# Pairs of 256-token expert tiles merged into tiles of 512 in a dilated attention and mixture-of-experts kernel

## The chip, the cores and the metric

The kernel runs on one core of one Trainium2 chip. The time is the device time of that core in microseconds (us), from the first to the last instruction with what lies around them; the median of three runs is given. The engines are PE (TensorE, matmuls; "PEld" is its weight load), DVE (VectorE), ACT (ScalarE), POOL (GpSimd) and SP (SyncE, which here only issues DMAs).

## The reference

Attention over 8 batches, 8 heads and 576 tokens gives rows `x` of 512 features; each token then goes through one of 8 experts. A token takes the expert of its own largest logit, or the one of the token before it, by a local gate. Only the second part matters here:

```
for b in range(B):                      # B, S, D, E, F = 8, 576, 512, 8, 1024
    prev_e = -1
    for s in range(S):
        fresh_e = int(np.argmax(logits[b, s]))
        if s == 0 or local_gate[b, s] < 0.5:  e = fresh_e
        else:                                 e = prev_e if prev_e >= 0 else fresh_e
        prev_e = e
        p = softmax(logits[b, s])
        h = np.maximum(x[b, s] @ w1[e], 0.0)
        out[b, s] = p[e] * (h @ w2[e])
```

All of it is f32. A matmul of f32 operands is two passes (two MATMUL records and two LDWEIGHTS records) in the trace.

## The kernel before, in words

**Stages.** Attention and routing take the first 181 us or so. While they run, each token's expert and place within that expert are worked out. Two units of 256 tokens (`EARLY`, `FIRST`) are formed from the first half of the batches; the rest is cut up once all tokens are routed (`count(True)`, `table`, `tokens`, lines 628 to 763). From there on the kernel is a list of *units*, `units` (lines 765 to 775): 14 of kind "pair" (256 tokens of one expert), 4 "full" (128 tokens), 1 "half" (64) and 3 "few" (32), in an order fixed at build time; only which tokens and which expert a unit holds is known at run time. With the two early ones there are 24 units.

**One unit.** `gather` fetches the token rows with indirect DMAs issued by POOL (two for each 128 tokens, into one of four `xg` buffers). `features` turns them with PE transposes and copies them to `xe` with ACT. `hidden` computes relu(x·w1) with the features on the partitions: the weights are PE's stationary operand, the tokens are the moving columns. `output` computes h·w2 with the tokens stationary and 256 of the 512 output features moving; the result is scaled by the gate into a `y` tile (three buffers), and `send` scatters 128 rows by an indirect DMA issued by POOL. Each send waits for the landing of the send before it, since both write `out`.

**Seven products in place of eight.** A pair is split 2×2 and multiplied by the Strassen-Winograd scheme in `chain` (lines 897 to 921). It needs sums of blocks of both operands: `sums_left` and `sums_right`, four DVE additions each. For the first product these are the sums of w1's blocks (`sums[0]`, 128x1024 each) and of the tokens (`xc`, 128x256); for the second, of h (`hc`, 128x512) and of w2's blocks (`sums[1]`, 128x1024). In `hidden` one of the seven products is 8 matmuls with 128 moving columns; in `output` it is 4 matmuls with 256.

**Order of the work.** PE, DVE, POOL and SP run in the order in which the program is written. The loop at line 1234 does, for unit u: `hidden(u)`, then `features(u + 1)`, `gather(u + 2)`, `output(u - 1)`. DVE's sums are slipped in between products, one or two at each `yield` of `chain` (`work_gap`, lines 817 to 821): during `hidden(u)` those for the output of u - 1 (`both`, line 1206), during `output(u - 1)` those of w1 for u + 1. The routing's last steps (`count`, `table`, `tokens`) are slipped in the same way between the products of unit 1's `hidden`, one step at each gap, each a short chain of DVE operations on 128x8 tiles.

**Weights.** There are three places for a unit's w1 and w2 (`raw1`, `raw2`, 2 MB each): pairs alternate between the first two, all other units use the third. A place is loaded for its next user as soon as its last reader is done (`weights`, lines 786 to 800; called from `run_hidden`, line 1193, and `run_output`, line 1201). The load is skipped where the place already holds the expert.

Of the kernel before, what the change touches and what calls it, by code (L numbers as in the profile page):

```python
# [81 lines left out]
PAIRS, FULL, HALF, FEWS = 14, 4, 1, 3  # L82
C_FULL, C_HALF, C_FEW = (2 * MOST + k * E for k in range(3))
COLS = C_FEW + E

# [133 lines left out]
def whole(ctx, tc, exact, bad, qk, v, wgl, w1, w2, con, adm, msk, qmk, out, cst, wg, ones, warm):  # L219
# [32 lines left out]
    def bank(shape, name):  # L252
        return banks.tile(shape, F32, name=name, tag="bank")
# [374 lines left out]
    def count(late):  # L628
# [11 lines left out]
        if late:  # L640
            ki, kf = number("ki", I32), number("kf")
            nc.vector.tensor_scalar(ki, ni, 5, None, Alu.logical_shift_right)
            nc.vector.tensor_scalar(ni, ni, float(FEW), None, Alu.add)
            tiles["over"] = over = sm.tile([1, 5], F32, name="over_late")
            most = sm.tile([1, 1], F32, name="most")
            nc.vector.tensor_reduce(most, cn[0:1], axis=AX.X, op=Alu.max)
            nc.vector.tensor_scalar(over[:, 4:], most, float(SEGS * P), None, Alu.is_gt)
# [3 lines left out]
        if late:  # L651

            nc.vector.tensor_copy(kf, ki)
            nc.vector.scalar_tensor_tensor(kf, nf, -8.0, kf, Alu.mult, Alu.add)
            full, half, few = number("full"), number("half"), number("few")
            nc.vector.tensor_scalar(full, kf, 3.0, None, Alu.is_ge)
            nc.vector.scalar_tensor_tensor(kf, full, -4.0, kf, Alu.mult, Alu.add)
            nc.vector.tensor_scalar(half, kf, 2.0, None, Alu.is_ge)
            nc.vector.tensor_scalar(few, kf, 1.0, None, Alu.is_equal)
            left = number("left")  # L660
            nc.vector.tensor_tensor(left, nf, tiles["done"], op=Alu.subtract)
            parts = [left, full, half, few]
# [6 lines left out]
        if late:  # L669
            for k, most in enumerate((PAIRS, FULL, HALF, FEWS)):  # L670
                nc.vector.tensor_scalar(over[:, k:k + 1], ends[k][0:1, E - 1:], float(most), None, Alu.is_gt)
        if not late:
            tiles["done"] = done = number("done")
            nc.vector.tensor_scalar(done, befs[0], -1.0, float(FIRST), Alu.mult, Alu.add)
            nc.vector.tensor_scalar(done, done, 0.0, None, Alu.max)
            nc.vector.tensor_tensor(done, done, nf, op=Alu.min)
            first, ends = None, [(done, befs[0], 0)]
        else:
            first = tiles["done"]
            nc.vector.tensor_tensor(befs[0], befs[0], first, op=Alu.subtract)  # L680
            ends = [(nf, befs[0], 0), (full, befs[1], C_FULL), (half, befs[2], C_HALF), (few, befs[3], C_FEW)]
        cols = COLS if late else 2 * FIRST
        tiles["chosen", late] = []
        for turn in range(PASSES if exact and late else 1):
# [7 lines left out]
            nc.vector.tensor_scalar(to, befs[0], 2.0, seg1, Alu.mult, Alu.add)  # L692
            if late:
                nc.vector.tensor_scalar(twice, first, 2.0, None, Alu.mult)
                nc.vector.scalar_tensor_tensor(to, twice, seg, to, Alu.is_le, Alu.mult)
# [28 lines left out]
    def tokens(late):  # L724
# [33 lines left out]
        if late:  # L758
            tiles["side"] = side = sm.tile([P, 2 * E], I32, name="side")
            for k, parts in enumerate((P // ROW, P // FEW)):  # L760
# [4 lines left out]
    n_pairs, *n_others = (MOST, E, E, E) if exact else (PAIRS, FULL, HALF, FEWS)  # L765
    others = [(kind, c + k) for k in range(max(n_others))
              for kind, c, most in zip(("full", "half", "few"), (C_FULL, C_HALF, C_FEW), n_others) if k < most]
    n_others = len(others)
    units = [dict(kind="pair" if i else "plain", col=2 * i, slot=i, late=False) for i in range(FIRST)]
    for k in range(n_pairs):  # L770
        i = k // 2 + k % 2 * (n_pairs // 2)
        units.append(dict(kind="pair", col=2 * i, slot=k % 2, late=True))
        while len(others) > min(n_others, max(n_others * (n_pairs - 1 - k) // (n_pairs - 2), k < n_pairs - 1)):
            kind, col = others.pop(0)
            units.append(dict(kind=kind, col=col, slot=2, late=True))
    NU = len(units)

    def of_unit(u, what, j=0, rows=P):
        return tiles[what, units[u]["late"]][:rows, units[u]["col"] + j:units[u]["col"] + j + 1]
# [43 lines left out]
    def now(push):  # L823
        for f in push:
            f()
# [32 lines left out]
    def tiles_of(u):  # L858
        return 2 if units[u]["kind"] in ("pair", "plain") else 1
# [21 lines left out]
    def features(u):  # L881
        kind = units[u]["kind"]
        rows = rows_in(u)
        xe[u] = mw.tile([P, DK, 2 * P], F32, name="xe")
        for j in range(tiles_of(u)):
            x = xg.pop((u, j)).rearrange("p g f -> p (g f)")
            tp = bank([P, DK, P], "tp")
            for kk in range(DK):
                nc.tensor.transpose(tp[:, kk, :rows], x[:rows, kk * P:(kk + 1) * P], ident[:rows, :rows])
            nc.scalar.copy(xe[u][:, :, j * P:j * P + rows], tp[:, :, :rows])  # L890
        if kind == "pair":
            xc[u] = mw.tile([P, 4, DK // 2, P], F32, name="xc", bufs=1)
            return sums_right(xc[u], *(xe[u][:, 2 * k:2 * k + 2, j * P:(j + 1) * P]
                                       for k in range(2) for j in range(2)))
        return []
# [27 lines left out]
    def hidden(u):  # L923
        i, kind = units[u]["slot"], units[u]["kind"]
        ht[u] = h = stage.tile([P, FK, 2 * P], F32, name="h", bufs=2)
# [36 lines left out]
        xyz = [bank([P, FK // 2, P], "hp") for _ in range(3)]  # L962

        def at(k):
            return h[:, k // 2 * FK // 2:(k // 2 + 1) * FK // 2, k % 2 * P:(k % 2 + 1) * P]

        def product(to, a, b, first):
            for m in range(FK // 2):
                for kk in range(DK // 2):
                    nc.tensor.matmul(to[:, m], lhsT=a[:, m, kk], rhs=b[:, kk], start=first and m == 0 and kk == 0,  # L970
                                     stop=(kk == DK // 2 - 1), skip_group_check=True)

        def keep(k, of):
            nc.scalar.copy(at((0, 1, 3)[k]), of)  # L974

        def finish(k, of):
            if k == 2:
                nc.scalar.activation(at(2), of, Act.Relu)
            else:
                nc.vector.tensor_tensor(at(k), of, at(k), op=Alu.add)  # L980
                nc.scalar.activation(at(k), at(k), Act.Relu)  # L981

        yield from chain((lambda i_, k: quarter(w, i_, k, False), lambda s: sums[0][:, s]),
                         (lambda k, j: x[:, 2 * k:2 * k + 2, j * P:(j + 1) * P], lambda s: xc[u][:, s]),
                         *xyz, product, keep, finish)
        units[u]["sums"] = sums_left(hc, at(0), at(2), at(1), at(3))
# [15 lines left out]
    def output(u):  # L1002
# [43 lines left out]
        xyz = [bank([P, D // 2], "yp") for _ in range(3)]  # L1046
        ys = [stage.tile([P, D], F32, name="y", bufs=3) for _ in range(2)]
        half = D // 2

        def product(to, a, b, first):  # L1050
            for m in range(FK // 2):
                nc.tensor.matmul(to, lhsT=a[:, m], rhs=b[:, m], start=first and m == 0,  # L1052
                                 stop=(m == FK // 2 - 1), skip_group_check=True)

        def at(k):
            return ys[k // 2][:, k % 2 * half:(k % 2 + 1) * half]

        def keep(k, of):
            k = (0, 1, 3)[k]
            nc.scalar.activation(at(k), of, Act.Copy, scale=of_unit(u, "gate", k // 2))  # L1060

        def finish(k, of):
            if k == 2:
                nc.scalar.activation(at(k), of, Act.Copy, scale=of_unit(u, "gate", 1))
                send(ys[1], u, 1)
            else:
                nc.vector.scalar_tensor_tensor(at(k), of, of_unit(u, "gate", k // 2), at(k), Alu.mult, Alu.add)  # L1067
                if k == 1:
                    send(ys[0], u, 0)

        yield from chain((lambda j, k: h[:, 4 * k:4 * k + 4, j * P:(j + 1) * P], lambda s: hc[:, s]),
                         (lambda k, j: quarter(w, k, j, True), lambda s: sums[1][:, s]),
                         *xyz, product, keep, finish)


    pause, rows = (None, 0, True), []

    def route(g, slow):
# [10 lines left out]
        if g in (EARLY - 1, NG - 1):  # L1089
# [6 lines left out]
            waiting.append(pause)  # L1096
# [61 lines left out]
    room(raw1, 2, "raw1", [P, FK, DK, P])  # L1158
    room(raw2, 2, "raw2", [P, FK, D])
# [43 lines left out]
    def is_pair(u):  # L1203
        return u < NU and units[u]["kind"] == "pair"

    def both(u):
        if not is_pair(u):
            return []
        return [f for two_ in zip(units[u]["sums"], sums_of_weights(u, True)) for f in two_]

# [22 lines left out]
    third = next(u for u in range(NU) if units[u]["slot"] == 2)  # L1233
    for u in range(FIRST, NU):
        run_hidden(u, both(u - 1) if u > FIRST else [])
# [4 lines left out]
        push = sums_of_weights(u + 1, False) if is_pair(u + 1) else []  # L1240
# [10 lines left out]
        if u == FIRST:  # L1251
            weights(third, False)
            weights(third, True)
# [4 lines left out]
    now(both(NU - 1))  # L1258
# [53 lines left out]
```

## Time and profile before

| what | us |
|---|---|
| median of 3 runs | 664.37 (662.84 to 665.11) |
| the profiled execution | 667.46 |
| its span, first to last instruction | 665.6 |
| span up to 181 us: attention and routing | PE busy 172.8 of 181.0 |
| 181 to 275 us | PE busy 92.0 of 94.0 |
| 275 us to the end | PE busy 381.8 of 390.6 |

The profile is one execution on the chip. A row of a timeline has the start, the length, engine, line, operation, output<-inputs, shape and number of merged instructions, and in brackets the idle time before it with what ended it. Ends of matmuls are modelled, so that a matmul's cost is read from the starts of successive rows, not from its length. In rows of groups, the numbers after the bar are the busy time of the group, the mean length of one in ns, and the idle time of the engine just before them.

### The profile page before, as it was taken

What the parts mean: (1) busy time and instruction counts of PE and PEld (TensorE: products, weight loads), DVE (VectorE), ACT (ScalarE), POOL (GpSimd) and SP (SyncE); (2) the same over time, 40 slices, a digit from 0 to 9 for tenths busy, and PEclk for the clock granted to TensorE, in tenths of its full rate; (3) what the DMA queues carried; (4) which work ended last, traced back from release to release, by engine and by line L of the source; (5) the groups of instructions that cost most, each with busy time, mean ns of one, the idle gap of its engine ahead of it and who ended that gap; (6) DMA issues with size and microseconds to landing.
All of it is one profiled execution on the core that took longest, in us unless ns stands there. A gap on an engine that the chain in (4) does not pass through costs nothing. (4 is left out here: it accounts for less than half of the span.)

```text
span 665.6 us, 15017 instructions
## 1 busy us (share of the span) xinstructions
PE 646.6 (97%) x6274; PEld 565.7 (85%) x6274; DVE 377.1 (57%) x787; ACT 193.9 (29%) x364; POOL 185.3 (28%) x169
## 2 busy tenths in 40 slices
PE   8999999989999999999999999999999999999996
PEld 6988888877588999999599888998899989899893
DVE  3558588682595595372537372718464537547440
ACT  3555454451112331222122222231222232223210
POOL 3322212250114420322542233323144213050011
PEclk9999999999999999999999999999999999999998
DMA  8999988849005397574633466541055451454001
GB/s 319 325 309 294 299 281 300 263 134 396 14 33 190 119 424 312 189 276 167 239 117 142 152 220 227 204 162 48 6 184 202 184 218 66 154 194 145 1 32 51
DMA packets 32686, 126.33 MB, mean 190 GB/s; under 512 B 8701, under 2 KB 17117, under 8 KB 28640
## 3 DMA queue, kind: packets, MB, share of 16 engines
q1 hardware_dynamic: 25808, 106.05, 44.2%
q0 software_dynamic: 6800, 19.21, 8.6%
q8 instruction: 52, 0.85, 0.5%
q14 instruction: 26, 0.21, 0.1%
HBM read 142.02 MB, written 19.20 MB: 242 GB/s over the span
## 5 line engine op out<-in xcount | busy, mean ns | idle before, releaser
L998 POOL DMA_INDIRECT out_dram<-y,tok x36 | 53.7, 1492 | 297.7 <-DVE y L1067 126.8
L970 PE MATMUL hp<-xc,sum 128*128 128x128 f32 x720 | 85.7, 276 | 0.7 <-DVE sum L837 0.7
L970 PEld LDWEIGHTS hp<-xc,sum 128*128 128x128 f32 x720 | 82.9, 192 | 1.2 <-PE hp L970 0.8
L1052 PE MATMUL yp<-sum,hc 128*128 128x256 f32 x360 | 82.6, 379 | 0.0
L980 DVE TENSOR_TENSOR h<-hp,h 128x512 f32<-128x512 f32 x45 | 30.9, 690 | 90.4 <-PE hp L970 90.4
L1052 PEld LDWEIGHTS yp<-sum,hc 128*128 128x128 f32 x360 | 68.4, 190 | 9.3
L1067 DVE SCALAR_TENSOR_TENSOR y<-yp,gate,y 128x256 f32<-128x256 f32 x45 | 21.7, 482 | 75.0 <-issue 49.0
L280 POOL COPY vt<-vt 32x1040 f32<-32x1040 f32 x32 | 34.3, 1074 | 92.9 <-DMA vt<-in_v_dram 61.5
L970 PE MATMUL hp<-xe,raw 128*128 128x128 f32 x480 | 58.8, 276 | 0.0
L970 PEld LDWEIGHTS hp<-xe,raw 128*128 128x128 f32 x480 | 56.6, 192 | 1.8 <-issue 1.5
L1052 PE MATMUL yp<-raw,h 128*128 128x256 f32 x240 | 57.1, 381 | 0.0
L335 PE MATMUL two<-kq 64*96 64x64 f32 x1152 | 53.3, 244 | 0.0
L874 POOL DMA_INDIRECT xg<-xd,tok x40 | 45.6, 1140 | 27.4 <-PE hp L970 14.4
L335 PEld LDWEIGHTS two<-kq 64*96 64x96 f32 x1152 | 53.1, 162 | 0.0
L974 ACT COPY h<-hp 128x512 f32<-128x512 f32 x45 | 26.4, 587 | 78.7 <-PE hp L970 73.9
L1052 PEld LDWEIGHTS yp<-raw,h 128*128 128x128 f32 x240 | 44.5, 190 | 5.5
L981 ACT ACTIVATE h<-h 128x512 f32<-128x512 f32 x45 | 28.3, 630 | 67.2 <-DVE h L980 58.2
L874 POOL DMA_INDIRECT xg<-xd,pos x40 | 43.5, 1088 | 11.8 <-issue 10.5
L340 DVE SCALAR_TENSOR_TENSOR pr<-two,mk 96x512 f32<-96x512 f32 x32 | 21.9, 683 | 38.1 <-ACT pr L342 26.4
L386 PE MATMUL pv<-vt,pr 96*64 96x65 f32 x1152 | 40.9, 224 | 0.0
L386 PEld LDWEIGHTS pv<-vt,pr 96*64 96x64 f32 x1152 | 36.4, 137 | 3.8 <-issue 1.2
L1060 ACT ACTIVATE y<-yp,gate 128x256 f32<-128x256 f32 x45 | 21.2, 474 | 54.7 <-PE yp L1052 50.7
(224 smaller groups left out, 1019.3 us busy)
## 6 DMA issues: line engine op xcount, KB each, us to landing
raw<-in_w_dram SPq DMA_DIRECT2D x48, 2048.0 KB
kq<-in_qk_dram SPq DMA_DIRECT2D x32, 592.0 KB
vt<-in_v_dram SPq DMA_DIRECT2D x32, 292.5 KB
xd<-x SPq DMA_DIRECT2D x16, 512.0 KB
raw<-in_w_dram SPq DMA_DIRECT2D x4, 512.0 KB
xd<-x SPq DMA_DIRECT2D x32, 32.0 KB
xg<-xd,tok POOLq DMA_INDIRECT x40
xg<-xd,pos POOLq DMA_INDIRECT x40
```

What stands on the lines that cost most here:

```text
L280: nc.gpsimd.tensor_copy(vt[:WIN, :, 1:], vt[QB:, :, :NB - 1])
L335: nc.tensor.matmul(sc[:KW, u, k * QB:(k + 1) * QB], lhsT=kt[h, i * QB:i * QB + KW], rhs=qt[h, i * QB:(i + 1) * QB], start=bool(late), stop ...
L340: nc.vector.scalar_tensor_tensor(pr, sc[:KW, :, :w], -CEIL, mk[:, kind].unsqueeze(1).to_broadcast([KW, 2, w]), Alu.max, Alu.min)
L386: nc.tensor.matmul(to[h * QB:(h + 1) * QB], lhsT=pr[i][:, u], rhs=vt[:, u, i], start=True, stop=True, tile_position=(0, h * QB), skip_grou ...
L874: nc.gpsimd.indirect_dma_start(out=x[:rows, g], out_offset=None, in_=xd[g] if units[u]["late"] else xd[g][:EARLY * GS], in_offset=bass.Ind ...
L970: nc.tensor.matmul(to[:, m], lhsT=a[:, m, kk], rhs=b[:, kk], start=first and m == 0 and kk == 0, stop=(kk == DK // 2 - 1), skip_group_chec ...
L974: nc.scalar.copy(at((0, 1, 3)[k]), of)
L980: nc.vector.tensor_tensor(at(k), of, at(k), op=Alu.add)
L981: nc.scalar.activation(at(k), at(k), Act.Relu)
L998: nc.gpsimd.indirect_dma_start(out=out, out_offset=bass.IndirectOffsetOnAxis(ap=of_unit(u, "tok", j), axis=0), in_=y, in_offset=None, boun ...
L1052: nc.tensor.matmul(to, lhsT=a[:, m], rhs=b[:, m], start=first and m == 0, stop=(m == FK // 2 - 1), skip_group_check=True)
L1067: nc.vector.scalar_tensor_tensor(at(k), of, of_unit(u, "gate", k // 2), at(k), Alu.mult, Alu.add)
```

## The change

The scheme, the tokens and the unit kinds "full", "half" and "few" stay. Twelve of the fourteen pairs become six units of a new kind, "quad", of 512 tokens; two pairs stay. A quad's `hidden` runs the same seven products with 256 moving columns instead of 128: each product's result takes two PSUM banks, and each copy, addition and relu is two instructions. Its `output` is the pair's output twice, for the first and the second 256 tokens (`q`), with the sums of h made anew for the second half just before it and the sums of w2 made once. The sums of w1 and of w2 are made once for 512 tokens. `xe`, `xc` and `h` of a quad have single buffers (`xeq`, `xcq`, `hq`).

The order of units is written out (`ORDER`). There are two weight places, the first for the first pair and all quads, the second for all others. The routing's `count` divides an expert's tiles into quads and pairs with some more DVE operations, and one more pause stands before `table`. Where a quad follows a unit that is neither pair nor quad, the sums of w2 are made during its own `hidden` (`early_sums`). The sums for the last unit are slipped into the output of the unit before it.

```diff
-PAIRS, FULL, HALF, FEWS = 14, 4, 1, 3
+QUADS, PAIRS, FULL, HALF, FEWS = 6, 2, 4, 1, 3
+ORDER = ("pair", "full", "quad", "few", "half", "quad", "full", "few", "quad", "full", "few", "quad", "pair", "quad",
+         "full", "quad")
...
-            parts = [left, full, half, few]
+            quads, pairs = number("quads"), number("pairs")
...
+                nc.vector.tensor_scalar(ki, left, 0.0, None, Alu.add)
+                nc.vector.tensor_scalar(ki, ki, 1, None, Alu.logical_shift_right)
+                nc.vector.tensor_copy(quads, ki)
+            nc.vector.scalar_tensor_tensor(pairs, quads, -2.0, left, Alu.mult, Alu.add)
+            parts = [quads, pairs, full, half, few]
...
-            nc.vector.tensor_tensor(befs[0], befs[0], first, op=Alu.subtract)
...
+            nc.vector.tensor_scalar(start, tiles["done"], 2.0, None, Alu.mult)
+            nc.vector.scalar_tensor_tensor(mid, quads, 4.0, start, Alu.mult, Alu.add)
+            nc.vector.scalar_tensor_tensor(base, befs[1], 2.0 if exact else -2.0, mid, Alu.mult, Alu.subtract)
+            nc.vector.tensor_scalar(base, base, 0.0 if exact else 2.0 * MOST - 2, None, Alu.add)
+            nc.vector.scalar_tensor_tensor(more, befs[0], 4.0, start, Alu.mult, Alu.subtract)
+            nc.vector.tensor_tensor(more, more, base, op=Alu.subtract)
...
+        units.append(dict(kind=kind, col=col, slot=k % 2 if exact else int(k > 0 and kind != "quad"), late=True))
...
-        xyz = [bank([P, FK // 2, P], "hp") for _ in range(3)]
+        t = tiles_of(u) * P // 2
+        parts = t // P
+        deep = FK // 2 // parts
+        xyz = [[bank([P, deep, t], "hp") for _ in range(parts)] for _ in range(3)]
...
         def product(to, a, b, first):
             for m in range(FK // 2):
+                part, m_ = divmod(m, deep)
                 for kk in range(DK // 2):
-                    nc.tensor.matmul(to[:, m], lhsT=a[:, m, kk], rhs=b[:, kk], start=first and m == 0 and kk == 0,
-                                     stop=(kk == DK // 2 - 1), skip_group_check=True)
+                    nc.tensor.matmul(to[part][:, m_], lhsT=a[:, m, kk], rhs=b[:, kk],
+                                     start=first and m_ == 0 and kk == 0, stop=(kk == DK // 2 - 1), skip_group_check=True)
...
+        for q in range(tiles_of(u) // 2):
+            if q:
+                now(sums_left(hc, *blocks(h, q)))
+            xyz = [bank([P, half], "yp") for _ in range(3)]
+            ys = [stage.tile([P, D], F32, name="y", bufs=3) for _ in range(2)]
...
-            waiting.append(pause)
+            waiting.extend([pause] * (1 + late))
...
-    room(raw1, 2, "raw1", [P, FK, DK, P])
-    room(raw2, 2, "raw2", [P, FK, D])
...
+    def early_sums(u):
+        if units[u]["kind"] != "quad" or u == FIRST or is_pair(u - 1):
+            return []
+        units[u]["ready"] = True
+        return sums_of_weights(u, True)
...
-        run_hidden(u, both(u - 1) if u > FIRST else [])
+        run_hidden(u, (both(u - 1) if u > FIRST else []) + early_sums(u))
...
-        push = sums_of_weights(u + 1, False) if is_pair(u + 1) else []
+        push = sums_of_weights(u + 1, False) if is_pair(u + 1) else both(u) if u + 1 == NU else []
```

## The prediction

> **What bounds the kernel now.** I read the page's busy times first, then the timeline of PE by stages, then PE's waits, then POOL at the end.
>
> ```profile
> PE 646.6 (97%) x6274; PEld 565.7 (85%) x6274; DVE 377.1 (57%) x787; ACT 193.9 (29%) x364; POOL 185.3 (28%) x169
> ```
>
> PE is busy 97% of the span, and the windows say the same of the expert stage (381.8 of 390.6 us). So the time is PE's work plus the few places where PE waits, plus what comes after PE's last matmul. DVE, ACT and the DMAs count only where one ends a wait of PE: DVE's additions of weights (the rows of `sum` show eight of 1.22 us for a pair) are not themselves on the path.
>
> What a matmul costs is read from the starts of rows in PE's timeline:
>
> ```profile
> 422.62 1.89 PE L1052 MATMUL yp<-raw,h 128*128 128x256 f32 x8
> ...
> 434.71 1.95 PE L970 MATMUL hp<-xe,raw 128*128 128x128 f32 x16
> ...
> 447.21 1.04 PE L889 MATMUL tp<-cst,xg 128*128 128x128 f32 x8
> ```
>
> From 422.62 to 434.71 is a pair's output: 56 passes (28 f32 matmuls, two passes each) in 12.09 us, 215.9 ns a pass of 256 columns. From 434.71 to 447.21 is a pair's hidden: 112 passes in 12.50 us, 111.6 ns a pass of 128 columns. Neither has a gap.
>
> **1. Wider matmuls: -4.9 us.** For 512 tokens, hidden is now 224 passes of 128 columns, 25.00 us. A quad needs 112 passes of 256 columns. The trace has this shape (128x128 weights, 256 moving) in output, so 112 x 215.9 = 24.18 us: 0.82 us for each of six quads. Output and transposes keep their number of passes. The gain is small because a pass is nearly in proportion to its columns: what the wider one saves is 2 x 111.6 - 215.9 = 7.3 ns, and 672 passes fall away. [...] These rows show weight loads that hide behind matmuls even at 128 columns, and I take the row. As 256 columns run without a gap in the same kernel, the term is firm: 4.5 to 5.2.
>
> **2. DVE's additions: -2.1 us.** Weight sums fall from 16 to 8 for 512 tokens: 6 x 8 x 1.22 = 59 us of DVE time. On PE's path this counts in two places:
>
> ```profile
> 242.68 2.05 PE L970 MATMUL hp<-xc,raw 128*128 128x128 f32 x16 [0.80 <-DVE h L980]
> ```
>
> ```profile
> 615.51 1.95 PE L970 MATMUL hp<-xe,sum 128*128 128x128 f32 x16
> 618.37 2.05 PE L970 MATMUL hp<-xc,raw 128*128 128x128 f32 x16 [0.91 <-DVE h L980]
> ```
>
> Both rows are of a pair's last product in hidden; what ended the wait is in the brackets. In the second, it should start 1.79 after 615.51, at 617.30, and starts at 618.37: 1.07 lost, as DVE reads that product's PSUM bank late, behind eight sums. The first lost 0.96 by the same reckoning. In the new order a pair with eight sums of its predecessor in its hidden doesn't occur: the two remaining pairs follow a unit of the early stage and a quad whose w2 sums are made already. In a quad a product lasts 3.45 us, against at most two sums (2.44 us), so nothing is late there. Bounds: 0 to 2.2.
>
> **3. The routing's chain: +1.1 us.** The late count gets 12 more DVE operations on 128x8 tiles: four for quads and pairs, one more scan, one difference, one comparison, six for the places less one removed. Such rows follow one another at 0.20 us where dependent and 0.08 where not; about 2.1 us. DVE has no idle time from 186.9 to 204.4, and PE is waiting at the end of it: the sum of h that unit 1's second output product needs ends just when that product starts.
>
> ```profile
> 203.77 0.68 DVE L837 TENSOR_TENSOR hc<-h 128x512 f32<-128x512 f32 x1
> ...
> 204.62 3.62 PE L1052 MATMUL yp<-sum,hc 128*128 128x256 f32 x16
> ...
> 212.42 0.72 PE L889 MATMUL tp<-cst,xg 128*128 128x128 f32 x4 [0.29 <-issue]
> ```
>
> So PE is held there by 2.0 us: at `table`, moved one product later, about 0.4 more than the 0.4 it waits now; at the last product of hidden, whose bank DVE reads late, and at the second product of output for the rest. Behind it on POOL the first late gathers move by 2.6. Two things give some back. The profile has a 2 MB load from 204 to 211 that holds those gathers (PE loses 0.5 at 212); in the new order unit 3 is of the expert that its place already holds, and the load is skipped. With the gathers earlier relative to PE, the wait for the first weight sum at 217 (0.68) shrinks by an estimated 0.4. Net 2.0 - 0.5 - 0.4 = 1.1; bounds 0.5 to 2.7.
>
> **4. The y tiles: +0.4 us.** A quad writes four y tiles but there are three. The second half's second tile is the first half's first, so ACT waits until that one's send has landed, and the fifth product of the second half needs what ACT does next. Counted from the start of the quad's output: the send starts at 10.36 (six products of 1.727) + 1.04 = 11.4; PE stalls if it lands after about 18.0 (fifth product at 12.09 + 6.91 = 19.0, less two ACT copies of 0.47). Sends that follow at once are some 3.7 apart (632.10 and 635.80), so it lands near 14.2. But under a weight load they take longer:
>
> ```profile
> 396.70 1.02 POOL L998 DMA_INDIRECT out_dram<-y,tok  x1 [6.00 <-DVE y L1067]
> 406.40 1.01 POOL L998 DMA_INDIRECT out_dram<-y,tok  x1 [8.68 <-ACT h L981]
> ```
>
> Here a load runs from 396.8 to 403.9, and the second send waits 9.7. [...] I laid out the new order's loads: at 11.4 of an output all are done, except in the first quad, where two queue (until about 12) and the eight gathers for the next quad stand before the send on POOL; there it lands near 18.4. The other gathers start up to a unit earlier, since three of their four buffers are free by then. Bounds 0 to 3.4 for each quad.
>
> **5. The end: +2.0 us.** Now the last unit is a "full":
>
> ```profile
> 651.33 0.98 POOL L998 DMA_INDIRECT out_dram<-y,tok  x1 [14.54 <-DVE y L1067]
> ...
> 652.02 7.03 PE L1040 MATMUL yp<-raw,h 128*128 128x512 f32 x16
> ...
> 656.83 0.99 POOL L998 DMA_INDIRECT out_dram<-y,tok  x1 [4.52 <-issue]
> ...
> 660.35 0.98 POOL L998 DMA_INDIRECT out_dram<-y,tok  x1 [2.53 <-DVE y L1043]
> ```
>
> Its matmuls end near 652.02 + 16 x 0.43 = 658.9, one send follows at 660.35 and the span ends at 665.6: 6.7 after PE. The new end is a quad's: two sends, the first ready one product (1.73) before PE's end, starting 1.04 after its product, that is 0.7 before PE's end; the second must wait for its landing, 3.7 (632.10) to 5.5 (651.33) later, and the end comes 5.2 after its start. That is 8.2 to 10.0 after PE, so +1.5 to +3.3; I take 2.0, nearer to the commoner spacing.
>
> **6. Costed at nothing.** Two weight places: a lone load takes 7 us and begins about 1 after its last reader. In the new order places alternate between a quad and others, and the tightest load (w1 of the first quad) has 11 us: the first pair's hidden ends, then a product, a full's hidden (7.1) and 16 transposes. w2 of that quad comes 8.3 into its hidden and holds DVE until then, but PE needs DVE only after four products, 13.8. Without such cover a load would cost up to 8. ACT and DVE have twice the instructions per product in a quad but also twice the time (1.3 of 3.45 us). The eight last sums move under the last full's output.
>
> **Sum:** -4.9 - 2.1 + 1.1 + 0.4 + 2.0 = -3.5 us. The profiled execution (667.46, span 665.6) would be 664.0; it lies 3.1 above the median of the runs shown, so the forecast for the median is 664.37 - 3.5 = **660.9**.
>
> **Rivals.** *Eaten up* (0.20): the routing's chain costs its full 2.7, the end 3.3, and one more gap like PE's 1.1 us of issue at 413.5 in a "few" unit: -4.9 - 2.1 + 2.7 + 0.4 + 3.3 + 1.1 = +0.5, 664.9. For it: DVE is full there. Against: the skipped load. *Sends hold the quads* (0.12): term 4 in the three quads before whose sends eight gathers stand, 3.4 each; from two stalled quads on the gain is gone. -3.9 + 3 x 3.4 = +6.3, 670.7. For it: 9.7 us between sends under a load. Against: the loads' places in the new order. *More* (0.10): chain 0.5, end 1.5, y 0, and the 1.1 gap gone: -6.1, 658.3. That the wide matmuls don't appear is excluded: the built program has them.
>
> **Numbers.** Forecast 0.58, with its own range 659.5 to 662.5. Runs of this kernel spread by 0.3%, 2 us, which is what a measurement can tell; faster by more means under 662.4. Forecast mostly (0.53), *more* all (0.10) and a little of *eaten up* (0.03): faster 0.66; same 0.21; slower 0.13. The range runs from *more* to just past *eaten up*, 657.5 to 665.0.
>
> **What would show it.** Quad hidden of 24.2 us; no PE wait on DVE h in pairs; hc in unit 1's output 2 us later; PE without a gap at a quad's twelfth output product; 8 to 10 us between PE's last matmul and the end. A gap of 3 us at that twelfth product, or passes of 256 columns over 220 ns in hidden, would make it wrong.

## The result, and the profile after

| kernel | median us | runs |
|---|---|---|
| before | 664.18 (661.54 to 665.30) | 6 |
| after | 657.46 (656.34 to 658.31) | 6 |

The ratio is 0.9902, with a 95% interval of 0.988 to 0.9924: 6.7 us faster, where 3.5 were forecast. The same two kernels were measured beside each other twice more, in the second and third set of experiments: 0.9939 (0.9917 to 0.996; 658.59 against 663.02) and 0.9909 (0.9878 to 0.994; 657.60 against 663.23). The three differences are 6.7, 4.4 and 5.6 us, so one set by itself says the size to little better than 2 us.

First the page of after, its busy times:

```profile
PE 637.7 (97%) x5602; PEld 542.1 (83%) x5602; DVE 323.0 (49%) x727; ACT 193.7 (30%) x364; POOL 172.9 (26%) x169
```

672 matmul records are gone and DVE works 54 us less, yet PE is busy for 97% as before: DVE's work shows in the time only where PE waited for it. Next, PE's timeline of after (start, length, engine, line, operation):

```profile
202.82 3.72 PE L1086 MATMUL yp<-sum,hc 128*128 128x256 f32 x16 [0.60 <-DVE hc L854]
...
301.79 1.89 PE L1086 MATMUL yp<-sum,hc 128*128 128x256 f32 x8
...
386.59 3.62 PE L995 MATMUL hp<-xeq,raw 128*128 128x256 f32 x16
...
410.77 0.60 PE L907 MATMUL tp<-cst,xg 128*128 128x128 f32 x4
...
492.07 1.95 PE L995 MATMUL hp<-xe,sum 128*128 128x128 f32 x16
493.86 1.95 PE L995 MATMUL hp<-xc,raw 128*128 128x128 f32 x16
```

A quad's hidden, from 386.59 to 410.77, takes 24.18 us. A pair's last product follows the one before it by 1.79, with no wait for h. PE waits 0.60 for `hc` at 202.82. The first quad's twelfth output product, at 301.79, has no idle time before it. And POOL's sends in the same trace, of the first quad and of the end:

```profile
294.19 1.21 POOL L1029 DMA_INDIRECT out_dram<-y,tok  x1 [1.35 <-DVE y L1104]
298.21 1.00 POOL L1029 DMA_INDIRECT out_dram<-y,tok  x1 [2.82 <-DMA out_dram<-y,tok]
...
645.85 0.99 POOL L1029 DMA_INDIRECT out_dram<-y,tok  x1 [7.42 <-DVE y L1104]
649.65 0.98 POOL L1029 DMA_INDIRECT out_dram<-y,tok  x1 [2.81 <-issue]
```

The first pair of sends is 4.0 apart, the last 3.8. PE's last matmul ends at 646.7 and the span at 654.6.

**A warning for reading the two profiled executions against each other.** Their spans differ by 11.0 us (665.6 and 654.6), more than the medians do. 3.7 of it lies before unit 1's hidden, in code that the change leaves alone: that hidden starts at 186.18 in the one and at 182.51 in the other. In the fourteen traces of this study it starts between 182.5 and 189.2, and both kernels spread. Up to 1.7 of the 3.7 is the clock: from 149.4 to 152.8 the granted clock is 0.5 in the trace of before, while PE is busy, and in after it is 1.0 there. Another 2.0 is a gap of PE in the trace of before, in the output of the first few, with no wait that the trace shows (PE's timeline of before):

```profile
410.65 1.17 PE L1012 MATMUL yp<-raw,h 128*32 128x128 f32 x33
412.07 0.31 PE L1012 MATMUL yp<-raw,h 128*32 128x128 f32 x2 [0.25 <-issue]
413.48 1.09 PE L1012 MATMUL yp<-raw,h 128*32 128x128 f32 x29 [1.10 <-issue]
```

These 64 records take 3.85 us up to the next unit's first matmul; the other fews' take 1.88. So a second profile of before was taken, and a like pair is compared further down.

### The profile page after: what moved, and what is told of

It reads as the page before. It is cut to its first block, busy times and chain, and to the rows that moved or that the text cites. A ratio compares the mean times of both kernels' runs of the same rounds, so it can differ in the third digit from the quotient of the medians.

```text
span 654.6 us, 13525 instructions
## 1 busy us (share of the span) xinstructions
PE 637.7 (97%) x5602; PEld 542.1 (83%) x5602; DVE 323.0 (49%) x727; ACT 193.7 (30%) x364; POOL 172.9 (26%) x169
## 2 busy tenths in 40 slices
DMA packets 32102, 117.83 MB, mean 180 GB/s; under 512 B 8637, under 2 KB 17053, under 8 KB 28576
## 5 line engine op out<-in xcount | busy, mean ns | idle before, releaser
L1029 POOL DMA_INDIRECT out_dram<-y,tok x36 | 44.0, 1223 | 262.8 <-DVE y L1104 99.4
L995 PE MATMUL hp<-xcq,sum 128*128 128x256 f32 x288 | 64.1, 379 | 0.0
L995 PEld LDWEIGHTS hp<-xcq,sum 128*128 128x128 f32 x288 | 54.7, 190 | 7.4
L1008 DVE TENSOR_TENSOR hq<-hp,hq 128x512 f32<-128x512 f32 x36 | 24.8, 690 | 52.6 <-PE hp L995 52.6
L1086 PE MATMUL yp<-raw,hq 128*128 128x256 f32 x192 | 45.7, 381 | 0.0
L995 PE MATMUL hp<-xeq,raw 128*128 128x256 f32 x192 | 43.5, 380 | 0.0
L1086 PEld LDWEIGHTS yp<-raw,hq 128*128 128x128 f32 x192 | 36.1, 190 | 5.3 <-issue 0.5
L995 PEld LDWEIGHTS hp<-xeq,raw 128*128 128x128 f32 x192 | 36.2, 190 | 4.8
L1097 ACT ACTIVATE y<-yp,gate 128x256 f32<-128x256 f32 x45 | 21.3, 473 | 63.6 <-PE yp L1086 58.7
L1009 ACT ACTIVATE hq<-hq 128x512 f32<-128x512 f32 x36 | 22.7, 630 | 44.1 <-DVE hq L1008 44.1
L1101 ACT ACTIVATE y<-yp,gate 128x256 f32<-128x256 f32 x15 | 7.1, 473 | 91.2 <-PE yp L1086 91.2
```

Source lines behind the costliest of these rows:

```text
L995: nc.tensor.matmul(to[part][:, m_], lhsT=a[:, m, kk], rhs=b[:, kk], start=first and m_ == 0 and kk == 0, stop=(kk == DK // 2 - 1), skip_gr ...
L1008: nc.vector.tensor_tensor(to, of[part], to, op=Alu.add)
L1009: nc.scalar.activation(to, to, Act.Relu)
L1029: nc.gpsimd.indirect_dma_start(out=out, out_offset=bass.IndirectOffsetOnAxis(ap=of_unit(u, "tok", j), axis=0), in_=y, in_offset=None, boun ...
L1097: nc.scalar.activation(at(k), of, Act.Copy, scale=gate(k))
```

## The experiments

They ran in four sets, each on one chip beside runs of the kernel before: narrow, half_sums, chain_ops, full_last; then after_again, later, before_again; then after_third, narrow_again, spaced; then half_again, chain_again. The median of before was 666.85, 663.02, 663.23 and 663.42 us in them.

### The widening alone: narrow and narrow_again

```diff
-                    nc.tensor.matmul(to[part][:, m_], lhsT=a[:, m, kk], rhs=b[:, kk],
-                                     start=first and m_ == 0 and kk == 0, stop=(kk == DK // 2 - 1), skip_group_check=True)
+                    for c in range(0, t, P):
+                        nc.tensor.matmul(to[part][:, m_, c:c + P], lhsT=a[:, m, kk], rhs=b[:, kk, c:c + P],
+                                         start=first and m_ == 0 and kk == 0 and c == 0, stop=(kk == DK // 2 - 1),
+                                         skip_group_check=True)
```

> The changed kernel with each matmul of a quad's hidden split into two of 128 moving columns: passes as before the change, everything else as after it. If the widening is worth what the rows of the pair say (7.3 ns for each of 672 removed passes), this is the changed kernel plus 4.9 us: 657.5 + 4.9 = 662.4, and a quad's hidden takes 25.0 us in place of 24.2. If the part of the gain that the forecast missed (3.2 us) comes from the widening too, it is 665 to 666, with gaps or waits of PE in the quads' hidden or longer passes.

Measured: 675.13, ratio 1.0122 (1.0088 to 1.0156) to before. That is far over the forecast's 662.4, of which 2.7 is the set's (before took 666.85 in it). Its trace, however, had 3.9 us of stall in the first quad's output (taken apart under full_last) and 6 more elsewhere, most of it in rows that the split doesn't touch, and full_last, in the same set, had the same stall. The changed kernel was not in the set, so this run settles nothing. It was repeated beside it:

> The kernel of narrow, unaltered, now beside the changed kernel. If the widening is worth 0.82 us for each quad, 4.9 over the changed kernel of this set, each quad's hidden 25.0 and every quad's output 24.2 to 24.4. In its first set it was 8 us over before, which with the changed kernel at 0.99 to 0.994 of before would be 12 to 15 over that: if 128 columns cost that much by themselves, it is 12 over again.

Measured: 662.66 (ratio 0.9992, 0.9977 to 1.0007) against 657.60 for the changed kernel: **5.06 us** for the widening. PE's timeline of narrow_again, the same quad as above:

```profile
389.77 3.74 PE L996 MATMUL hp<-xeq,raw 128*128 128x128 f32 x32
...
414.78 0.60 PE L907 MATMUL tp<-cst,xg 128*128 128x128 f32 x4
```

25.01 us in place of 24.18. Over six quads the rows sum to 150.26 and 145.25 (in after_third): 5.0. All other rows are alike to 0.02 us. A removed pass is worth 5.06 / 672 = 7.5 ns, where the rows of before had given 7.3.

### DVE's additions alone: half_sums and half_again

In `sums_of_weights` of the kernel before:

```diff
         assert (u, second) in loads
+        if units[u]["late"] and i == (0 if second else 1):
+            return []
...
```

Where a pair has no such sums, the ones of h are made alone.

> The kernel before, without the sums of w2 for the seven late pairs in the first weight place and without the sums of w1 for the seven in the second: 56 additions of 1.22 us less on DVE (the output is not the reference's). If DVE matters only where PE waited for h in two pairs, it gains 2.0 us by the forecast, 2.6 by the length of those two hiddens (13.83 and 13.78 against 12.50): 661.6 to 662.2. If the freed DVE also quickens PE elsewhere (shorter passes, no gap in a few's output), 4 us or more: 660 and less.

Measured: 663.57, ratio 0.9955 (0.994 to 0.997), 3.3 us less than before's 666.85. PE's two hiddens were 12.50 and 12.61, but the first few's output was 4.28 there.

> The kernel of half_sums, unaltered (56 additions of weights left out of the kernel before), to be read against a profile of before in which PE has no gap in the first few's output. If only the two pairs gain, its two hiddens are 12.5 to 12.6 in place of 13.82 and 13.78, every other row of PE is as in before, and the time is 2.6 less; 2.0 by the forecast's reckoning.

Measured: 660.40, ratio 0.9949 (0.9929 to 0.9968), 3.0 less. PE's timeline of half_again at the first of the two places:

```profile
236.60 1.95 PE L972 MATMUL hp<-xe,sum 128*128 128x128 f32 x16
238.39 1.95 PE L972 MATMUL hp<-xc,raw 128*128 128x128 f32 x16
```

and of before_again at the same place, with the start of unit 1's output above it and the first few's output below:

```profile
203.28 3.62 PE L1052 MATMUL yp<-sum,hc 128*128 128x256 f32 x16
...
210.19 0.60 PE L889 MATMUL tp<-cst,xg 128*128 128x128 f32 x4
211.25 0.70 PE L889 MATMUL tp<-cst,xg 128*128 128x128 f32 x4 [0.47 <-DMA xg<-xd,tok]
...
238.41 1.95 PE L970 MATMUL hp<-xe,sum 128*128 128x128 f32 x16
241.16 2.05 PE L970 MATMUL hp<-xc,raw 128*128 128x128 f32 x16 [0.80 <-DVE h L980]
...
409.14 1.96 PE L1012 MATMUL yp<-raw,h 128*32 128x128 f32 x64
```

In before the last product starts 2.75 after the one ahead of it, without the sums 1.79. From unit 1's hidden to PE's last matmul it is 468.05 us in half_again and 470.64 in before_again: 2.59 for 68 us of DVE work, and 2.49 of that are these two hiddens (13.82 to 12.50, 13.78 to 12.61). Nothing else on PE grew faster by more than 0.1 with an idler DVE. The end after PE's last matmul is 0.4 shorter (5.99 against 6.38), which makes up the 3.0.

### The routing's chain alone: chain_ops and chain_again

The kernel before with the change's twelve extra DVE operations (four for quads and pairs, a scan, a difference, a comparison and five more), whose results nothing uses, and with its one more pause.

```diff
+            nc.vector.tensor_scalar(ki, left, 0.0, None, Alu.add)
+            nc.vector.tensor_scalar(ki, ki, 1, None, Alu.logical_shift_right)
...
-            waiting.append(pause)
+            waiting.extend([pause] * (1 + late))
```

> The kernel before with the change's twelve more operations in the late count and its one more pause before the table, the results of the operations unused. The load from 204 to 211 us stays. By the forecast PE is held 2.0 us and 0.4 come back at the first weight sum: before + 1.6 = 665.8, with the second product of unit 1's second output kind 2.0 us later after its hidden. If DVE's chain is hidden by PE's products, 0 to 0.5: 664.5. If the gathers behind it collide with loads, 2.7 or more: 667.

Measured: 670.70, ratio 1.0058 (1.0035 to 1.0081): 3.9 us. From unit 1's hidden to the end of the first late pair's hidden it took 44.4 us, 2.6 more than in a quiet trace of before.

> The kernel of chain_ops, unaltered (twelve more operations and one more pause in the kernel before, which keeps its load from 204 to 211 us). From unit 1's hidden to the end of the first late pair's hidden it was 44.4 us where before has 41.8 to 42.0 and the changed kernel 43.1. If the skipped load is what gives the changed kernel 1.3 back, it is 44.4 again, and the time is before + 2.6; if the first set was disturbed there too, 43.4 and before + 1.6, as the forecast has it.

Measured: 664.51, ratio 1.0022 (1.0002 to 1.0042): 1.1 us. The stretch is 42.96, against 41.79 in before_again and 43.09 in after_third: +1.17 here, +1.30 in the changed kernel. PE's timeline of chain_again:

```profile
205.05 3.72 PE L1068 MATMUL yp<-sum,hc 128*128 128x256 f32 x16 [0.61 <-DVE hc L853]
```

Unit 1's hidden starts at 184.92 here and at 184.84 in before_again, where this product is at 203.28: PE is held 1.7 us. 0.6 comes back where before waits for a gather at 211.25, though this kernel keeps its load. So the skipped load isn't needed for this give-back. In both kernels the gathers land behind the load, whose last packet ends 25.53 us after unit 1's hidden began in before_again and 26.45 in chain_again: PE is 1.7 later, the load only 0.9. The expectation of 44.4 or 43.4 was a miss to the low side.

### The end: full_last and later

```diff
-ORDER = ("pair", "full", "quad", "few", "half", "quad", "full", "few", "quad", "full", "few", "quad", "pair", "quad",
-         "full", "quad")
+ORDER = ("pair", "full", "quad", "few", "half", "quad", "full", "few", "quad", "few", "quad", "pair", "quad",
+         "full", "quad", "full")
```

> The changed kernel with the order's last full behind the last quad in place of before the fourth: pair full quad few half quad full few quad few quad pair quad full quad full. If the end after PE's last matmul is what the change pays for ending on a quad (8.05 us in its trace against 6.7 before), this is 1.35 faster than the changed kernel: 656.1, with one send behind PE's end. If the second send of the last quad still runs under the full's output and its landing holds the last one, 0 to 0.5 faster. If the fourth quad's w2 load, which now starts with that quad's hidden, holds PE, it is 1 to 8 slower.

Measured: 668.45, ratio 1.0025 (1.0009 to 1.0042). The end was right (6.2 us after PE's last matmul), the total a miss by 12, of which 2.7 is again the set's. DVE's timeline of full_last, at the first quad's output, where its program is still that of after:

```profile
293.46 0.48 DVE L1104 SCALAR_TENSOR_TENSOR y<-yp,gate,y 128x256 f32<-128x256 f32 x1 [7.97 <-issue]
296.33 0.88 DVE L1104 SCALAR_TENSOR_TENSOR y<-yp,gate,y 128x256 f32<-128x256 f32 x2 [2.38 <-PE yp L1086]
```

and of after:

```profile
289.96 0.48 DVE L1104 SCALAR_TENSOR_TENSOR y<-yp,gate,y 128x256 f32<-128x256 f32 x1 [6.14 <-issue]
291.69 0.48 DVE L1104 SCALAR_TENSOR_TENSOR y<-yp,gate,y 128x256 f32<-128x256 f32 x1 [1.25 <-PE yp L1086]
```

Counted from the start of that output (284.36 and 282.69) DVE takes up these results at 9.1 and 12.0 in the one, at 7.3 and 9.0 in the other, though PE had made them at the same point. PE's timeline of full_last shows that this is only half of the stall:

```profile
293.10 1.89 PE L1086 MATMUL yp<-raw,hc 128*128 128x256 f32 x8
296.87 2.59 PE L1086 MATMUL yp<-sum,hq 128*128 128x256 f32 x8 [1.88 <-DVE y L1104]
299.24 3.03 PE L1086 MATMUL yp<-raw,hq 128*128 128x256 f32 x8
302.11 3.62 PE L1086 MATMUL yp<-sum,hc 128*128 128x256 f32 x16
```

The product at 296.87 is 2.0 late because PE waits for DVE. The two products from there on then take 2.37 and 2.87 in place of 1.73, 1.8 more, because the granted clock is 0.5 from 298.1 to 301.5. The stall of narrow has the same two parts (a wait of 1.92, then 0.5 from 300.8 to 304.2). Whether DVE's lateness belongs to the kernel was the question of the next set.

> The changed kernel, unaltered, beside the others of this set. If the change is worth what its first runs say on any day, 0.990 of the kernel before, with every quad's output 24.2 to 24.4 us; then the order with the full last is 8 us slower by its own doing. If the changed kernel has a place that is late on some days (in the order with the full last, whose first half is the same program, the first quad's output took 28.1 us because DVE's second copy of y came 3 us late), its median is within 2 us of before and its first quad's output is 28 us here too.

Measured: 658.59, ratio 0.9939 (0.9917 to 0.996); the first quad's output took 24.28. So that stall is not the program's.

> The kernel before, unaltered, for a second profile: 666.9 with the median of the last set, 664.2 with that of the first. If PE's gap of 2.0 us in the first few's output (3.85 against 1.88) belongs to the kernel, it is here again, as it was in both variants of the kernel before; if it comes with the day, it may be gone.

Measured: 663.65 in its one run; the first few's output took 1.88 (its row is shown above), so the gap of 2.0 isn't the program's either.

The next kernel has full_last's order, and besides the count's six comparisons in `check`, five units later:

```diff
-            nc.vector.tensor_scalar(over[:, 5:], most, float(SEGS * P), None, Alu.is_gt)
+            later.append((5, most, SEGS * P))
...
-                nc.vector.tensor_scalar(over[:, k:k + 1], ends[k][0:1, E - 1:], float(most), None, Alu.is_gt)
+                later.append((k, ends[k][0:1, E - 1:], most))
...
+        for k, of, limit in tiles["later"]:
+            nc.vector.tensor_scalar(tiles["over"][:, k:k + 1], of, float(limit), None, Alu.is_gt)
```

> The order with the full last, and besides the count's six comparisons (one element each) made in the later check instead of between the scan and the table. Six operations of 0.08 to 0.2 us leave the chain that PE waits for behind unit 1's hidden: 0.5 to 1.2 us faster than the order with the full last alone (668.45, or 1.0025 of before). Against the changed kernel of the same set: 1.35 + 0.8 = 2.2 faster if the order costs nothing by itself; 6 to 7 slower if the order is what made full_last slow.

Measured: 661.80, ratio 0.9979 (0.9965 to 0.9993): 6.7 less than full_last, but in another set, and 3.2 more than the changed kernel beside it. So the order costs by itself. POOL's timeline of later:

```profile
412.96 0.94 POOL L892 DMA_INDIRECT xg<-xd,tok  x1 [12.31 <-PE tp L908]
414.20 0.94 POOL L892 DMA_INDIRECT xg<-xd,pos  x1 [0.30 <-issue]
```

and PE's:

```profile
412.25 0.43 PE L908 MATMUL tp<-cst,xg 32*128 32x32 f32 x4
...
416.23 1.53 PE L908 MATMUL tp<-cst,xg 128*128 128x128 f32 x12
420.40 0.66 PE L908 MATMUL tp<-cst,xg 128*128 128x128 f32 x2 [2.65 <-DMA xg<-xd,tok]
422.13 0.69 PE L908 MATMUL tp<-cst,xg 128*128 128x128 f32 x2 [1.07 <-DMA xg<-xd,pos]
422.62 3.62 PE L1087 MATMUL yp<-raw,hq 128*128 128x256 f32 x8
426.03 4.05 PE L1087 MATMUL yp<-sum,hc 128*128 128x256 f32 x16
429.92 1.89 PE L1087 MATMUL yp<-raw,hq 128*128 128x256 f32 x8
```

The lone few between two quads holds one of four `xg` buffers until its transposes at 412.25; the quad's fourth tile can be fetched only then, and is wanted 4 us later, beside two weight loads. It costs 4.6 us at the transposes and 1.9 in the output that follows. The 1.9 is the clock, which is granted at 0.5 from 420.1 to 426.9: the product at 422.62 takes 3.41 in place of 1.73, and the two at 426.03 take 3.89 in place of 3.45. The first expectation had looked for the trouble at the weights; it was at the gathers. The six deferred comparisons bring 0.3 us (29.63 against 29.93 from unit 1's hidden to the first late pair's), less than the 0.5 to 1.2 expected.

### An order that keeps both: spaced

This has later's comparisons and another order; after_third, in the same set, is the changed kernel once more.

```diff
+ORDER = ("pair", "full", "quad", "few", "half", "quad", "full", "quad", "pair", "quad", "few", "quad", "full",
+         "few", "quad", "full")
```

> The changed kernel, unaltered, as the measure for the other two of this set. 0.990 to 0.994 of before by the two sets so far; PE from unit 1's hidden to its last matmul 464.2 us as in both its traces.

Measured: 657.60, ratio 0.9909 (0.9878 to 0.994), and 464.20 us from unit 1's hidden to PE's last matmul.

> The six comparisons in the later check, and an order that ends on a full with no lone few between two quads unless a pair stands before the first of them: pair full quad few half quad full quad pair quad few quad full few quad full. If the 4.6 us that PE waited for a quad's last gathers at 416 us in later, and the 1.9 in the quad after it, came from the lone few behind a quad behind a few, they are gone, and the end's 1.9 and the chain's 0.3 remain: the changed kernel of this set - 2.2. If ending on a full costs by itself, it is no faster than the changed kernel.

Measured: **655.80**, ratio 0.9882 (0.9849 to 0.9914), 1.8 less than the changed kernel beside it, which is close to the 2.2 expected and the fastest median of the study; no interval was taken between the two. POOL's timeline of spaced:

```profile
645.54 0.99 POOL L1030 DMA_INDIRECT out_dram<-y,tok  x1 [3.94 <-ACTq L218]
649.41 0.98 POOL L1030 DMA_INDIRECT out_dram<-y,tok  x1 [2.87 <-DVE y L1075]
```

PE's last matmul ends at 648.35. The last quad's second send, at 645.54, runs under the full's output, one send follows PE's end, and the span ends at 654.3: 5.9 after PE, where after_third has 8.3. The waits for gathers are gone, and with them the slow clock behind them: it is 1.0 until PE's end.

## Why the prediction was right, point by point

The pair to compare is before_again and after_third, two traces without gaps of the kind just shown. Starts of PE's rows, in us:

| stretch | before | after | difference |
|---|---|---|---|
| unit 1's hidden to the end of the first late pair's | 41.79 | 43.09 | +1.30 |
| hidden of the other 13 pairs; of one pair and six quads | 165.64 | 157.86 | -7.78 |
| all other rows of PE | 263.21 | 263.25 | +0.04 |
| PE's last matmul to the end of the span | 6.38 | 8.33 | +1.95 |
| sum | 477.02 | 472.53 | -4.49 |

- **1, wider matmuls, -4.9.** Right: 5.0 by the rows, 5.06 by the medians.
- **2, DVE's additions, -2.1.** Right in place, short in size: 2.5 by the two hiddens, 2.6 by half_again's rows. The working took the delay of the last product's start alone (0.96 and 1.07); the smaller slips around the other products of the same hidden, 0.36 and 0.10, were left out. The length of the whole hidden against an undisturbed one would have given them.
- **3, the chain, +1.1.** +1.30. Of its parts, PE was held 2.0 as foretold: unit 1's output reaches its transposes 27.33 us after unit 1's hidden began, in before_again 25.35. The give-back was 0.7 at these transposes (0.87 long in after_third, 1.60 in before_again), not 0.5, and nothing at the first weight sum, not 0.4.
- **4, the y tiles, +0.4.** Mis-sized: 0. The send was at 11.5 of the output as laid out, but the two loads had ended at 294.1, just as it began, and not later; it landed at 14.7 of the output, where the working has 14.2 without a load and 18.4 with one, and the next followed 4.0 after it, not 7. What a load does to a send was right: under later loads of the same trace sends land only 7.5 and 9.2 after their start (306.27 and 314.52), where the one at 294.19 took 3.2. In none of the quiet traces is there a gap at the twelfth product.
- **5, the end, +2.0.** +1.95 in this pair; 7.85, 8.67 and 8.33 after PE in the three traces of after, 6.53 and 6.38 in the two of before.
- **6, costed at nothing.** The rows outside hidden differ by 0.04 in sum, so the loads in two places, ACT and the last sums cost nothing in sum, as forecast.

The table sums to -4.5, the forecast to -3.5. Of the difference, term 2 makes 0.4, term 4 makes 0.4 and term 1 makes 0.1; small slips of the other hiddens, which the change cuts and no term held, make 0.3; term 3 takes 0.2 back. So the misses add up and don't cancel: the sign rests on term 1 and was not luck. The -4.5 is within the second and the third measurement (2.7 to 5.5 and 4.0 to 8.1 faster, from the intervals) and 0.5 short of the edge of the first (5.0 to 8.0). The first set's extra two microseconds are not settled: its median, 657.46, lies under the forecast's own 659.5 to 662.5 and nearer to the rival *more* (658.3). Of what *more* counted on, the y tiles came true, the chain (1.3, not 0.5) and the end (1.95, not 1.5) did not. The 2.0 us gap in the first few, the last of its grounds, is in the one trace of before from that day; but that it was in the runs behind the median isn't shown. *Eaten up* fell by term 3 (1.3, not 2.7) and term 5. *Sends hold the quads* fell because no quad's output is over 24.4 us.

## What to carry to other kernels

Here matmuls of 128 columns already ran with no gap, and widening them to 256 brought 7.5 ns by the medians for each pass that fell away, 7.3 by the rows of before (two passes of 111.6 ns against one of 215.9). Where you think of widening, measure the start-to-start time of both shapes in the same trace, and multiply the difference by the passes that fall away. A cut in another engine's work was worth only the waits it ended (2.59 us for 68 us of DVE's work), but count them over the whole stage that contains them, not by the bracket of one row. When an order of work is changed, look which buffers a short unit holds between two long ones, and what stands between the last result and the end. A stall can cost more than its wait (1.8 us on top of 2.0 in full_last): read the granted clock just behind it.

## What the runs showed of the hardware

**A slower clock behind a wait.** Three traces have a wait of PE of 1.88 us or more in the expert stage, and in each the granted clock goes to 0.5, in later while PE still waits, in the other two 1.3 us or less after the wait: for 3.4 us in narrow and full_last, for 6.8 in later. The longest wait there without this is 1.69, in chain_ops. The matmuls in such a stretch take twice as long (3.41 us for a product of 1.73 in later), and in full_last that cost 1.8 on top of a wait that cost 2.0. What decides is not shown: at 144 us of the attention a wait of 1.2 us comes just before such a stretch in before_again, and one as long has none behind it in half_again.

**Late engines and missing records.** Five traces (before and the first set) have places where an engine goes on late with no wait that the trace shows: 2.0 us and more in a few's output (3.85 in before, with two weight loads issued from 410.31 on), whose 64 matmuls otherwise take 1.88, and DVE up to 3 us late for a finished product (12.0 us into the output in full_last, 9.0 in after). In the same five the trace holds 3,555 to 3,794 records of landed transfers; the nine without such places hold 4,279 to 4,359, for nearly the same transfers (before has 3,794 beside 32,686 DMA packets, after 4,279 beside 32,102). So missing records and late engines came together, in variants of both kernels (before, half_sums and chain_ops; narrow and full_last). Whether the one has to do with the other is not shown, nor what causes either; the whole first set ran on one chip. What it means for reading: a comparison of two traces is safe only if both have it or both lack it, and the kernel to compare with belongs in the same set. Narrow by itself, 1.0122 against the changed kernel's first 0.9902, would have put the widening at 15 us, three times its worth.
